# First three weight tiles loaded ahead of the first chunk, another order of the first eight steps' pieces, zeros in wider matmuls

## Chip, cores, metric

One core of a Trainium2 chip (trn2). The metric is device microseconds (us) of one execution; every kernel ran several times, and ratios compare its runs with runs of the kernel before on the same chip. In the profiles PE is TensorE (PEld its weight loads), DVE VectorE, ACT ScalarE, POOL GpSimd, and SP issues the loads; "share" of DMA is that of 16 engines.

## The reference, cut to what matters

```python
# retention: per head, a decayed state; q, k, v are (4, 8, 768, 64), float32
for t in range(S):
    state = gamma[None, :, None, None] * state + np.einsum('bhd,bhe->bhde', k[:, :, t], v[:, :, t])
    y[:, :, t] = scale * np.einsum('bhd,bhde->bhe', q[:, :, t], state)
x = y.transpose(0, 2, 1, 3).reshape(3072, 512)
# feed-forward; w_in is (512, 2048), w_out (2048, 512), both float64
h = x @ w_in
return ((h - np.tanh(h)) @ w_out).astype(np.float32)
```

## The kernel before

The sequence is cut into 24 chunks of 128 tokens. A chunk is turned (q and k transposed, on PE for the first eight chunks), multiplied into scores and state products with 32 small matmuls, masked, and put out as x. The feed-forward runs in 96 steps of an up product, a chain on ACT and DVE, and a down product two steps later. The weights come as float64 in 32 tiles: each is converted by two instructions on ACT, four on DVE and a last two on DVE or GpSimd. The first eight steps and eight chunks are written out as a list of pieces. A letter names the piece, a number its chunk, tile or step:

```python
pieces = {
    "L": load_chunk, "W": load_weights,
    "s": lambda c: scale(c, 0, tall(c)),          # q of a chunk, on DVE or GpSimd
    "w": lambda c: scale(c, 1, tall(c)),          # v of a chunk
    "t": ..., "T": ...,                           # PE transposes of k, of q
    "c": ..., "C": ...,                           # ACT copies of these
    "p": products, "m": mask, "z": state,         # PE, DVE, DVE
    "b": outputs, "r": outputs_rest, "y": keep_x, # PE, PE, ACT ("e": ACT reads y once)
    "A": convert_begin, "D": convert_bits,        # a weight tile: ACT, DVE
    "G": lambda i: convert_end(i, tall(i)),       # and its end: DVE or GpSimd
    "u": ..., "v": ...,                           # up product, first and second half
    "a": ..., "q": ..., "d": ..., "g": ...,       # its chain on ACT, ACT, DVE, DVE
    "o": ..., "E": ...,                           # down product, its sum
    "x": lambda n: idle.__setitem__(0, n),        # n matmuls of zeros before the next group
}

def keep_busy(at):
    for _ in range(idle[0]):
        nc.tensor.matmul(at, busy, busy, start=True, stop=True, skip_group_check=True)
    idle[0] = 0

# in load_chunk: k and q of a chunk have two buffers, v has four
t = inp.tile([P, H, D], F32, tag=nm, name=f"{nm}_{ci}", bufs=4 if nm == "v" else 2)
```

A piece's instructions go to their engine in the order of the list, and every engine works in its own order. The float32 matmuls are two PE instructions each, a transpose is one.

Of the kernel before, what the change touches and what calls it, by code (L numbers as in the profile page):

```python
# [16 lines left out]
P = 128  # L17
# [7 lines left out]
B0, C0 = 1.1162213056058772, 5.494931718829769  # L25
B1, C1 = -1.609711559785289, 5.546157850574988
# [6 lines left out]
def kernel(  # L33
# [20 lines left out]
    nc = tc.nc  # L54
# [28 lines left out]
    def bank(tag, name):  # L83
        return ps.tile([P, BANK], F32, tag=tag, name=name)

    def banks(tag, name):

        return ps.tile([P, 2, BANK], F32, tag=tag, name=name, bufs=1)
# [4 lines left out]
    at = [0]  # L93
# [6 lines left out]
    busy = cst.tile([P, P], F32, name="busy")  # L100
# [9 lines left out]
    w1 = wts.tile([P, NC, DF], F32, name="w1")  # L110
    w2 = wts.tile([P, NM, DM], F32, name="w2")
# [78 lines left out]
    def convert_end(i, engine):  # L190
        if i not in words:
            return
        dst, src = weight_ends(i)
        head, low, power = words.pop(i)
        engine.tensor_tensor(low, low, power.bitcast(F32), op=ALU.mult)  # L195
        head = head.bitcast(F32)
        if isinstance(src, list):
            low, head = (t.rearrange("p (c n) -> p c n", c=NC) for t in (low, head))
        engine.tensor_tensor(dst, low, head, op=ALU.add)  # L199
# [5 lines left out]



    idle = [0]

    def keep_busy(at):  # L210
        for _ in range(idle[0]):
            nc.tensor.matmul(at, busy, busy, start=True, stop=True, skip_group_check=True)  # L212
        idle[0] = 0


    loaded = {}
# [15 lines left out]
    def scale(ci, which, engine):  # L232
        if ci >= NCH:
            return
        t, g = loaded[ci][1 + which], (gq, gv)[which]
        engine.tensor_tensor(t, t, g[:, ts(ci % CPB, H)][:, :, None].to_broadcast([P, H, D]),  # L236
                             op=ALU.mult)

    def turn(ci, which, early=False):

        if early:
            tp = bank("o", f"kqTp{which}_{ci}")
        else:
            if which == 0:
                turned[ci] = banks("t", f"kqTp_{ci}")
            tp = turned[ci][:, which]
        keep_busy(tp[:, :P])
        t = loaded[ci][which]
        for p in range(NP):
            nc.tensor.transpose(tp[:, ts(p, P)],  # L250
                                t[:, ds(2 * p, 2)].rearrange("p h d -> p (h d)"), ident)
        if early:
            turned.setdefault(ci, []).append(tp)
# [31 lines left out]
    scores = {}  # L285

    def products(ci):

        kh, _, vh = loaded[ci]
        kT, qT = (sides[ci][:, i] for i in range(2))  # L290
        sp = banks("t", f"s_{ci}")
        keep_busy(sp[:, 0, :P])
        scores[ci] = halves = sp.rearrange("p r (w n t) -> p r w n t", w=2, n=NP)
        for p in range(NP):
            for a in range(2):
                for i in range(2):
                    h, r = 2 * p + i, ds(D * a, D)
                    nc.tensor.matmul(halves[ds(D * i, D), a, 1, p], kh[r, h], vh[r, h],  # L298
                                     start=True, stop=True, skip_group_check=True)
        for p in range(NP):  # L300
            for a in range(2):
                for i in range(2):
                    r = ds(D * i, D)
                    nc.tensor.matmul(halves[ds(D * a, D), i, 0, p], kT[r, p, ts(a, D)],  # L304
                                     qT[r, p, ts(a, D)], start=True, stop=True,
                                     skip_group_check=True)
# [7 lines left out]
        masked[ci] = m  # L314

    def state(ci):
        halves = scores.pop(ci)
        j = ci % CPB
        if j == 0:
            states[ci] = mid.tile([P, 2, NP, D], F32, tag="state", name=f"state_{ci}", bufs=3)  # L320
            nc.vector.tensor_copy(states[ci][:, 1], halves[:, 0, 1])
        else:
            nc.vector.tensor_tensor(states[ci][:, 1], halves[:, 0, 1], states[ci][:, 0],
                                    op=ALU.add)
        if j < CPB - 1:
            nxt = mid.tile([P, 2, NP, D], F32, tag="state", name=f"state_{ci + 1}", bufs=3)
            nc.vector.tensor_tensor(nxt[:, 0], halves[:, 1, 1], states[ci][:, 1], op=ALU.add)
            states[ci + 1] = nxt
# [7 lines left out]
    def outputs(ci):  # L336

        j = ci % CPB
        vh = loaded[ci][2]
        turned.pop(ci, None)  # L340
        qT = sides.pop(ci)[:, 1]
        a_, st = masked.pop(ci), states.pop(ci)
        y = y_banks[:, ci % 2]
        keep_busy(y[:, 0, 0])
        begun = set()

        def to_y(p, i, a, lhsT, rhs):

            col, r = (i + p) % 2, (ci + p) % 2
            start = (r, col) not in begun  # L350
            begun.add((r, col))
            nc.tensor.matmul(y[ds(D * col, D), r, p // 2, ts(a, D)], lhsT, rhs,  # L352
                             start=start, stop=True, skip_group_check=True)

        def intra(first):
            for pp in range(NP // 2):
                for i in range(2):
                    for a in range(2):

                        for col in range(2):  # L360
                            p = 2 * pp + ((a + col) % 2 if first else (a + col + 1) % 2)
                            if (i + p) % 2 != col:
                                continue
                            r = ds(D * a, D)
                            to_y(p, i, a, vh[r, 2 * p + i], a_[r, i, p])

        for a in range(2):
            if j or a:
                for p in range(NP):
                    for i in range(2):  # L370
                        r = ds(D * i, D)
                        to_y(p, i, a, st[r, a, p], qT[r, p, ts(a, D)])
        intra(True)
        halfway[ci] = intra
# [25 lines left out]
    o_p = {}  # L400
# [6 lines left out]
    def up(n, m2, i):  # L407

        if i == 0:
            hps[n, m2] = bank("h", f"h_{n}_{m2}")  # L410
        hp = hps[n, m2][:, ts(i, TH)]
        keep_busy(hp[:, :P])
        for c in range(NC):
            nc.tensor.matmul(hp, w1[:, c, ts(2 * m2 + i, P)], xT[n // 2][:, c, ts(n % 2, TH)],  # L414
                             start=(i == 0 and c == 0), stop=(c == NC - 1),
                             skip_group_check=True)
# [39 lines left out]
    def down(n, m2, j, first, last):  # L456

        if first:
            o_p[j] = bank("o", f"o_{n}_{m2}_{j}")
            keep_busy(o_p[j][:, :P])  # L460
        for i in range(2):
            nc.tensor.matmul(o_p[j], gT[n, m2][:, i, ts(j, P)], w2[:, 2 * m2 + i],  # L462
                             start=(first and i == 0), stop=(last and i == 1))
# [74 lines left out]

    BEGUN = 8
    EARLY_TURNS = 4  # L540
    TO_VECTOR = 2

    def tall(ci):
        return nc.vector if ci < TO_VECTOR else nc.gpsimd

    pieces = {
        "L": load_chunk,
        "W": load_weights,
        "s": lambda c: scale(c, 0, tall(c)),
        "w": lambda c: scale(c, 1, tall(c)),  # L550
        "t": lambda c: turn(c, 0, c < EARLY_TURNS),
        "T": lambda c: turn(c, 1, c < EARLY_TURNS),
        "c": lambda c: turn_copy(c, 0),
# [7 lines left out]
        "y": keep_x,  # L561
        "A": convert_begin,
        "D": convert_bits,
        "G": lambda i: convert_end(i, tall(i)),
        "u": lambda s: up(*steps[s][:2], 0),
        "v": lambda s: up(*steps[s][:2], 1),
        "a": lambda s: shrink_begin(*steps[s][:2]),
# [3 lines left out]
        "o": lambda s: [down(*steps[s][:2], j, *steps[s][2:]) for j in range(2)],  # L571
        "E": lambda s: [add_up(*steps[s][:2], j) for j in range(2)],
        "x": lambda n: idle.__setitem__(0, n),
    }
    if w_out.dtype != F32:
        rooms += [xp.tile([P, 2, 2 * BANK], U32, tag="xT", name=f"raws_{i}") for i in range(3)]
    order = """
    L0 x8 t0 c0 s0 x5 T0 w0 L1 C0 x3 t1 W0 p0 c1 s1 m0 x2 T1 z0 W1 C1 w1 x3 b0 p1 e0 A0 r0
    m1 z1 y0 A1 D0 L2 x4 b1 t2 e1 c2 G0 r1 s2 y1 D1 x3 T2 w2 L3 u0 C2 W2 p2 G1 s3 t3 m2 T3
    w3 c3 v0 z2 C3 b2 A2 L4 p3 e2 W3 D2 a0 r2 s4 y2 w4 q0 W4 m3 z3 G2 x9 t4 b3 A3 d0 T4 e3  # L580
    C4 r3 g0 L5 y3 x1 p4 A4 W5 u2 D3 s5 v2 W6 w5 m4 D4 u1 G3 a2 q2 z4 L6 x6 t5 d2 G4 T5 A5
    v1 W7 C5 g2 b4 s6 a1 W8 p5 w6 e4 u3 D5 q1 v3 m5 A6 G5 z5 r4 L7 a3 t6 d1 b5 W9 y4 T6 e5
    o0 s7 g1 C6 w7 A7 W10 D6 q3 r5 t7 W11 T7 D7 G6 y5 C7 x3 u4 d3 v4 G7 A8 g3 p6 a4 o1 A9 m6
    z6 q4 D8 p7 E1 d4 G8 b6 o2 e6 m7 g4 A10 r6 z7 u5 y6 D9 b7 v5 D10 G9 e7 r7 a5 o3 y7 q5
    G10 u6 E3 d5 A11 v6 g5 o4 a6 D11 q6 u7 G11 d6 v7 g6 o5 a7 q7 E5 d7 g7 W12 L8 W13 W14
    """
    for piece in order.split():
        pieces[piece[0]](int(piece[1:]))
# [10 lines left out]
    for s in range(BEGUN, len(steps)):  # L599
        n, m2, first, last = steps[s]  # L600
        ci = with_chunk.get(s)
# [86 lines left out]
```

## Time and profile before

| | us |
|---|---|
| Time | 752.62, median of 3 (752.61 to 753.97) |
| PE busy | 740.9 (99% of the span of 752.1) |
| First useful transposes | 4.6 |
| First up product (u0) | 20.3 |
| Step 8, from where nothing is changed | 98.7 |
| Last up product | 734.06 |

The time is from the runs, PE's busy time from the page, the others from PE's timeline.

### The profile page before, as it was taken

Reading aid. Unit: us, or ns where it says so; the run is one execution under the profiler, and the core shown is the slowest. Engines: PE = TensorE matmul, PEld = TensorE weight load, DVE = VectorE, ACT = ScalarE, POOL = GpSimd, SP = SyncE. Lnnn points to the kernel's source line nnn. Section 1 sums busy time; section 2 is a strip of 40 time slices with the busy share of each in tenths; the row PEclk is TensorE's granted clock in tenths of the full one; section 3 lists DMA queues with packets and bytes.
Section 4 is the critical chain, followed back from the end, with each engine's and each line's share of the span. In section 5 each row is a group of like instructions: output and inputs, shape, how many; then the busy total and the mean of one; then the engine's idle time right before and its main releaser. Section 6 shows DMA issues by size and latency. Waiting matters only on the chain.

```text
span 752.1 us, 13885 instructions
## 1 busy us (share of the span) xinstructions
PE 740.9 (99%) x5502; PEld 509.9 (68%) x5502; DVE 518.0 (69%) x807; ACT 389.4 (52%) x727; POOL 126.9 (17%) x108
## 2 busy tenths in 40 slices
PE   8899999999999999999999999999999999999997
PEld 7786667666767676766676676666666666666775
DVE  4889989998898666656565656565665666656653
ACT  4567576667665546445545545444344434434442
POOL 0565445445444111100111100000000000000000
PEclk9999999999999999999999999999999999999999
DMA  9972436556553353343342421000000000000000
GB/s 196 234 182 74 127 89 172 158 158 153 156 128 84 99 155 107 67 96 93 91 99 71 98 58 56 29 1 1 29 0 1 28 1 0 29 0 1 28 2 28
DMA packets 125680, 59.76 MB, mean 79 GB/s; under 512 B 109872, under 2 KB 118576, under 8 KB 125616
## 3 DMA queue, kind: packets, MB, share of 16 engines
q1 hardware_dynamic: 125328, 58.67, 29.9%
q8 instruction: 43, 0.70, 0.4%
q10 hardware_dynamic: 288, 0.21, 0.1%
q14 instruction: 21, 0.17, 0.1%
HBM read 35.80 MB, written 14.68 MB: 67 GB/s over the span
## 4 chain that ended last, share of the span: by engine, by line
PE 96%; DMA 2%; DVE 1%; SPq 1%; ACT 0%; issue 0%; ACTq 0%; DVEq 0%
PE h L414 44%; PE o L462 42%; PE y L352 3%; PE o L470 2%; PE s L298 2%; PE s L304 1%; PE kqTp L212 1%; PE kqTp L250 1%; DMA raw<-in_moe_w_in_dram 1%; DMA k<-in_k_dram 1%; SPq L229 1%; DMA out_dram<-sum 0%; SPq L154 0%; DVE power L187 0%; DVE head L185 0%; DVE a L311 0%
## 5 line engine op out<-in xcount | busy, mean ns | idle before, releaser
L414 PE MATMUL h<-xT,w 128*128 128x256 f32 x1536 | 349.9, 381 | 0.0
L414 PEld LDWEIGHTS h<-xT,w 128*128 128x128 f32 x1536 | 289.7, 190 | 68.4 <-issue 31.8
L462 PE MATMUL o<-w,g 128*128 128x512 f32 x736 | 331.9, 593 | 0.0
L462 PEld LDWEIGHTS o<-w,g 128*128 128x128 f32 x736 | 139.4, 190 | 135.1 <-issue 128.4
L423 ACT ACTIVATE u<-h 128x512 f32<-128x512 f32 x96 | 57.3, 597 | 289.0 <-PE h L414 288.9
L439 DVE TENSOR_TENSOR th<-h,th 128x512 f32<-128x512 f32 x96 | 66.3, 690 | 176.0 <-ACT th L424 176.0
L453 DVE COPY_PREDICATED g<-large,th 128x512 f32<-128x512 int32 x96 | 71.8, 748 | 10.2 <-DVE g L452 0.5
L442 DVE SCALAR_TENSOR_TENSOR h<-q,h 128x512 f32<-128x512 f32 x96 | 66.8, 696 | 10.4 <-DVE h L440 0.5
L448 DVE SCALAR_TENSOR_TENSOR h<-q,h 128x512 f32<-128x512 f32 x96 | 66.6, 694 | 8.2
L431 ACT ACTIVATE q<-u,tab 128x512 f32<-128x512 f32 x96 | 69.4, 722 | 0.0
L432 ACT ACTIVATE q<-u,tab 128x512 f32<-128x512 f32 x96 | 69.1, 720 | 0.0
L433 ACT ACTIVATE large<-u,tab 128x512 f32<-128x512 f32 x96 | 68.8, 717 | 0.0
L452 DVE TENSOR_TENSOR g<-h,u 128x512 f32<-128x512 f32 x96 | 66.3, 691 | 3.3
L440 DVE SCALAR_TENSOR_TENSOR h<-u,h 128x512 f32<-128x512 f32 x96 | 65.8, 685 | 0.0
L236 POOL TENSOR_TENSOR q<-q,tab 128x512 f32<-128x512 f32 x22 | 24.3, 1104 | 198.4 <-DMA q<-in_q_dram 115.1
L424 ACT ACTIVATE th<-h 128x512 f32<-128x512 f32 x96 | 56.9, 592 | 0.0
L195 POOL TENSOR_TENSOR low<-low,power 128x512 f32<-128x512 f32 x30 | 38.5, 1282 | 103.1 <-DVE power L187 89.1
L199 POOL TENSOR_TENSOR w<-low,head 128x512 f32<-128x512 f32 x30 | 38.7, 1289 | 2.4
L352 PEld LDWEIGHTS y<-a,v 64*64 64x64 f32 x768 | 15.8, 134 | 16.7 <-ACT large L433 10.6
L236 POOL TENSOR_TENSOR v<-v,tab 128x512 f32<-128x512 f32 x22 | 26.5, 1207 | 0.1
L382 ACT COPY seen<-y 64x1 f32<-64x1 f32 x96 | 10.1, 153 | 28.2 <-PE y L352 27.8
L393 ACT COPY xT<-y 128x512 f32<-128x512 f32 x24 | 14.1, 587 | 17.0 <-PE y L352 17.0
(54 smaller groups left out, 412.8 us busy)
## 6 DMA issues: line engine op xcount, KB each, us to landing
rows<-apart SPq DMA_DIRECT2D x16, 512.0 KB, 2.8
k<-in_k_dram SPq DMA_DIRECT2D x24, 256.0 KB, 4.3
q<-in_q_dram SPq DMA_DIRECT2D x24, 256.0 KB, 4.9
v<-in_v_dram SPq DMA_DIRECT2D x24, 256.0 KB, 5.1
raw<-in_moe_w_out_dram SPq DMA_DIRECT2D x12, 512.0 KB, 3.6
out_dram<-sum SPq DMA_DIRECT2D x23, 256.0 KB, 2.1
raw<-in_moe_w_in_dram SPq DMA_DIRECT2D x14, 256.0 KB, 4.2
raw<-in_moe_w_in_dram SPq DMA_DIRECT2D x28, 128.0 KB, 3.9
```

The costliest lines, as they stand in the source:

```text
L414: nc.tensor.matmul(hp, w1[:, c, ts(2 * m2 + i, P)], xT[n // 2][:, c, ts(n % 2, TH)], start=(i == 0 and c == 0), stop=(c == NC - 1), skip_g ...
L423: nc.scalar.activation(u, hp, AF.Square)
L431: nc.scalar.activation(q0, u, AF.Square, bias=bias0)
L432: nc.scalar.activation(q1, u, AF.Square, bias=bias1, scale=math.sqrt(A))
L433: nc.scalar.activation(large, u, AF.Relu, bias=bias_m)
L439: nc.vector.tensor_tensor(th, hp, th, op=ALU.subtract)
L440: nc.vector.scalar_tensor_tensor(hp, in0=u, scalar=R, in1=hp, op0=ALU.subtract, op1=ALU.mult, reverse0=True)
L442: nc.vector.scalar_tensor_tensor(hp, in0=q0, scalar=C0, in1=hp, op0=ALU.add, op1=ALU.mult)
L448: nc.vector.scalar_tensor_tensor(hp, in0=q1, scalar=A * C1, in1=hp, op0=ALU.add, op1=ALU.mult)
L452: nc.vector.tensor_tensor(flat, hp, u, op=ALU.mult)
L453: nc.vector.copy_predicated(flat, large.bitcast(I32), th)
L462: nc.tensor.matmul(o_p[j], gT[n, m2][:, i, ts(j, P)], w2[:, 2 * m2 + i], start=(first and i == 0), stop=(last and i == 1))
```

## The change

The intent: load and convert three weight tiles while nothing else can run, so that DVE is not stopped later by a tile that comes late; take out the zeros that stand between useful matmuls later; and make the rest cheaper by 512-column matmuls. It also moves the scales of chunk 1 from DVE to GpSimd and those of chunk 4 from GpSimd to DVE. The core of the diff:

```diff
     def keep_busy(at):
-        for _ in range(idle[0]):
-            nc.tensor.matmul(at, busy, busy, start=True, stop=True, skip_group_check=True)
-        idle[0] = 0
+        most = at.shape[-1] // P
+        while idle[0]:
+            n = min(idle[0], most)
+            zeros = busy[:, None, :].to_broadcast([P, n, P])
+            nc.tensor.matmul(at[:, : n * P].rearrange("p (n t) -> p n t", n=n), busy, zeros,
+                             start=True, stop=True, skip_group_check=True)
+            idle[0] -= n
...
-    TO_VECTOR = 2        # scales and tile ends 0 and 1 on DVE, the others on GpSimd
+    SCALED = {0, 4}      # scales of these chunks on DVE
+    ENDED = {0, 1}       # ends of these tiles on DVE
...
+        "X": lambda n: (idle.__setitem__(0, n), keep_busy(bank("h", "zeros"))),
...
     order = """
-    L0 x8 t0 c0 s0 x5 T0 w0 L1 C0 x3 t1 W0 p0 c1 s1 m0 x2 T1 z0 W1 C1 w1 x3 b0 p1 e0 A0 r0
-    m1 z1 y0 A1 D0 L2 x4 b1 t2 e1 c2 G0 r1 s2 y1 D1 x3 T2 w2 L3 u0 C2 W2 p2 G1 s3 t3 m2 T3
-    w3 c3 v0 z2 C3 b2 A2 L4 p3 e2 W3 D2 a0 r2 s4 y2 w4 q0 W4 m3 z3 G2 x9 t4 b3 A3 d0 T4 e3
-    C4 r3 g0 L5 y3 x1 p4 A4 W5 u2 D3 s5 v2 W6 w5 m4 D4 u1 G3 a2 q2 z4 L6 x6 t5 d2 G4 T5 A5
     ... (four more lines)
+    W0 W1 W2 A0 D0 L0 A1 G0 D1 A2 L1 D2 X40 t0 W3 c0 s0 w0 X7 T0 t1 G1 C0 p0 c1 s1 z0 L2 m0
+    w1 X3 T1 b0 G2 e0 C1 p1 z1 A3 r0 L3 m1 t2 y0 D3 W4 c2 b1 s2 e1 X1 r1 T2 w2 y1 C2 X2 p2
+    s3 t3 m2 c3 z2 w3 L4 T3 b2 W5 C3 G3 p3 e2 A4 r2 m3 u0 z3 y2 L5 s4 t4 D4 b3 T4 v0 C4 w4
+    e3 r3 p4 y3 z4 s5 a0 u2 m4 q0 G4 L6 d0 W6 t5 W7 b4 A5 T5 w5 g0 v2 W8 C5 e4 u1 a2 D5 W9
     ... (four more lines, ending in "A11 o5 g7 D11 E5 G11")
     """
```

More of the change, by code (lines that the diff above doesn't have):

```diff
@@ L246, in turn @@
             tp = turned[ci][:, which]
-        keep_busy(tp[:, :P])
+        keep_busy(tp)
         t = loaded[ci][which]
@@ L291, in products @@
         sp = banks("t", f"s_{ci}")
-        keep_busy(sp[:, 0, :P])
+        keep_busy(sp[:, 0])
         scores[ci] = halves = sp.rearrange("p r (w n t) -> p r w n t", w=2, n=NP)
@@ L316, in state @@
     def state(ci):
-        halves = scores.pop(ci)
+        halves = scores[ci]
         j = ci % CPB
@@ L343, in outputs @@
         y = y_banks[:, ci % 2]
-        keep_busy(y[:, 0, 0])
         begun = set()
@@ L411, in up @@
         hp = hps[n, m2][:, ts(i, TH)]
-        keep_busy(hp[:, :P])
+        keep_busy(hp)
         for c in range(NC):
@@ L459, in down @@
             o_p[j] = bank("o", f"o_{n}_{m2}_{j}")
-            keep_busy(o_p[j][:, :P])
+            keep_busy(o_p[j])
         for i in range(2):
@@ L540, with engine @@
     EARLY_TURNS = 4
-    TO_VECTOR = 2
-    def tall(ci):
-        return nc.vector if ci < TO_VECTOR else nc.gpsimd
+    SCALED = {0, 4}
+    ENDED = {0, 1}
+    def engine(i, among):
+        return nc.vector if i in among else nc.gpsimd
     pieces = {
@@ L548 @@
         "W": load_weights,
-        "s": lambda c: scale(c, 0, tall(c)),
-        "w": lambda c: scale(c, 1, tall(c)),
+        "s": lambda c: scale(c, 0, engine(c, SCALED)),
+        "w": lambda c: scale(c, 1, engine(c, SCALED)),
         "t": lambda c: turn(c, 0, c < EARLY_TURNS),
@@ L563 @@
         "D": convert_bits,
-        "G": lambda i: convert_end(i, tall(i)),
+        "G": lambda i: convert_end(i, engine(i, ENDED)),
         "u": lambda s: up(*steps[s][:2], 0),
@@ L577 @@
     order = """
-    L0 x8 t0 c0 s0 x5 T0 w0 L1 C0 x3 t1 W0 p0 c1 s1 m0 x2 T1 z0 W1 C1 w1 x3 b0 p1 e0 A0 r0
-    m1 z1 y0 A1 D0 L2 x4 b1 t2 e1 c2 G0 r1 s2 y1 D1 x3 T2 w2 L3 u0 C2 W2 p2 G1 s3 t3 m2 T3
-    w3 c3 v0 z2 C3 b2 A2 L4 p3 e2 W3 D2 a0 r2 s4 y2 w4 q0 W4 m3 z3 G2 x9 t4 b3 A3 d0 T4 e3
-    C4 r3 g0 L5 y3 x1 p4 A4 W5 u2 D3 s5 v2 W6 w5 m4 D4 u1 G3 a2 q2 z4 L6 x6 t5 d2 G4 T5 A5
-    v1 W7 C5 g2 b4 s6 a1 W8 p5 w6 e4 u3 D5 q1 v3 m5 A6 G5 z5 r4 L7 a3 t6 d1 b5 W9 y4 T6 e5
-    o0 s7 g1 C6 w7 A7 W10 D6 q3 r5 t7 W11 T7 D7 G6 y5 C7 x3 u4 d3 v4 G7 A8 g3 p6 a4 o1 A9 m6
-    z6 q4 D8 p7 E1 d4 G8 b6 o2 e6 m7 g4 A10 r6 z7 u5 y6 D9 b7 v5 D10 G9 e7 r7 a5 o3 y7 q5
-    G10 u6 E3 d5 A11 v6 g5 o4 a6 D11 q6 u7 G11 d6 v7 g6 o5 a7 q7 E5 d7 g7 W12 L8 W13 W14
+    W0 W1 W2 A0 D0 L0 A1 G0 D1 A2 L1 D2 X40 t0 W3 c0 s0 w0 X7 T0 t1 G1 C0 p0 c1 s1 z0 L2 m0
+    w1 X3 T1 b0 G2 e0 C1 p1 z1 A3 r0 L3 m1 t2 y0 D3 W4 c2 b1 s2 e1 X1 r1 T2 w2 y1 C2 X2 p2
+    s3 t3 m2 c3 z2 w3 L4 T3 b2 W5 C3 G3 p3 e2 A4 r2 m3 u0 z3 y2 L5 s4 t4 D4 b3 T4 v0 C4 w4
+    e3 r3 p4 y3 z4 s5 a0 u2 m4 q0 G4 L6 d0 W6 t5 W7 b4 A5 T5 w5 g0 v2 W8 C5 e4 u1 a2 D5 W9
+    q2 p5 z5 G5 r4 v1 y4 m5 d2 b5 a1 s6 t6 o0 e5 L7 g2 w6 A6 W10 q1 D6 T6 W11 u3 C6 d1 s7 p6
+    w7 r5 v3 z6 y5 G6 A7 m6 g1 t7 b6 T7 u4 C7 D7 e6 a3 p7 z7 G7 A8 r6 v4 m7 y6 q3 d3 b7 o1
+    a4 g3 A9 q4 d4 u5 e7 g4 r7 v5 y7 E1 u6 D8 a5 q5 o2 d5 G8 g5 A10 v6 D9 u7 a6 q6 o3 D10 d6
+    G10 v7 E3 g6 G9 o4 a7 q7 d7 A11 o5 g7 D11 E5 G11 W12 L8 W13 W14
     """
```

## The prediction

> **What bounds the kernel now.** I read the page first, then the chain of work that ended last, then a table of stretches, the PE's waits, and the timelines of PE, DVE, DMA issues and GpSimd over the first 100 us, which is all that the change touches.
>
> ```profile
> PE 740.9 (99%) x5502; PEld 509.9 (68%) x5502; DVE 518.0 (69%) x807; ACT 389.4 (52%) x727; POOL 126.9 (17%) x108
> PE   8899999999999999999999999999999999999997
> DMA  9972436556553353343342421000000000000000
> ```
>
> PE is busy 99% of the span, and the chain is 96% PE. From 98.87 us on it is an unbroken alternation of 3.45 us (sixteen up matmuls) and 3.43 us (eight down matmuls) with chunk work between; those 653 us the change does not touch. So only PE time before 98.87 us can be won. The table of stretches says where it is (us, then busy time of PE, PEld, DVE, ACT, POOL, clock, DMA share, GB/s):
>
> ```profile
> 0.00:8.00 8.00, 6.71 (x40) 6.28 (x40) 1.55 (x3) 2.45 (x3) 0.20 (x4) 1.00 0.99 175
> 8.00:16.00 8.00, 5.77 (x194) 5.11 (x194) 5.16 (x11) 3.35 (x9) 0.00 (x0) 1.00 1.19 236
> 16.00:28.50 12.50, 12.23 (x302) 10.41 (x302) 10.33 (x16) 6.56 (x19) 5.31 (x5) 1.00 0.93 208
> 28.50:38.30 9.80, 6.21 (x92) 5.62 (x90) 9.28 (x15) 5.62 (x14) 7.00 (x6) 0.83 0.92 253
> 38.30:84.90 46.60, 46.58 (x652) 33.69 (x653) 43.19 (x67) 31.28 (x66) 25.07 (x21) 1.00 0.49 126
> ```
>
> After 38.3 us PE idles no more (46.58 of 46.60), though DVE is 93% busy beside it. Before 38.3 us the DMA engines are full (share 0.9 and more) and PE has holes. The large one, in PE's timeline and its waits:
>
> ```profile
> 28.05 0.46 PE L352 MATMUL y<-a,v 64*64 64x64 f32 x16
> 31.45 3.60 PE L212 MATMUL kqTp<-busy 128*128 128x128 f32 x18 [2.94 <-DVE state L327]
> 34.84 0.93 PE L250 MATMUL kqTp<-tab,k 128*128 128x128 f32 x4
> PE kqTp L212 <- DVE state L327: 2.9, 1, 2.9
> ```
>
> PE waits 2.94 us, then runs 3.6 us of zeros (L212) before it does anything useful: 6.3 us. What it waits for is the state of chunk 3 on DVE, and DVE is late because it stands in order behind the conversion of the third weight tile:
>
> ```profile
> 27.12 0.43 DVE L181 TENSOR_SCALAR head<-head 128x512 f32<-128x512 f32 x1 [1.66 <-ACT head L172]
> 28.77 1.15 DVE L187 TENSOR_SCALAR power<-head 128x512 uint32<-128x512 uint32 x1
> 19.34 2.38 SPq L154 DMA_DIRECT2D raw<-in_moe_w_in_dram x3
> 26.40 0.69 ACT head L172
> ```
>
> That tile was issued at 19.34 us, behind four chunks, and landed at 26.3. So the chain of the hole is DMA, ACT, four DVE instructions, mask and state of chunk 3, PE.
>
> **What the Trainium skill says.** "SBUF — State Buffer", section "Who interferes with whom", says that VectorE and GpSimd share a port pair by an exclusive lock, so one fully blocks. The trace agrees: the bit operations of a conversion take 0.43 us alone, and 1.15 to 1.39 us beside a GpSimd instruction (28.77 above; GpSimd scales chunk 4 then). I count 13 such cases before 90 us, some 11 us of DVE. "TensorE: Matmul & The Clock Gate", Part 1, says that the clock is halved at the start and after about 3.4 us without work. The trace agrees roughly: the first 16 zero instructions take 3.78 us, later ten take 1.28, and the clock of 30 to 35 us is 0.71 after the 2.9 us hole. "DMA: Bandwidth & Descriptors", section "Why small descriptors are slow (HBM only)", says that 256-byte descriptors pay a fixed overhead. The trace agrees: 218 GB/s at 5 to 8 us, where all 2586 packets are under 512 bytes (chunks), and 250 GB/s at 8 to 11 us, where w_in's come in.
>
> **The change, part by part.** Units: a chunk is three loads of 262 KB, a weight tile 524 KB.
>
> *1. Three weight tiles first.* The new DMA order is W0 W1 W2, chunk 0, chunk 1, W3, chunk 2, chunk 3, W4, chunk 4, W5. What PE can do first is delayed. Chunk loads land 1.2 us apart (chunk 1's k released PE at 8.14 us, its q DVE at 9.34). A w_in tile costs 2.0 us at 260 GB/s; by landings it costs more, as cumulative bytes over landing times hold near 198 GB/s (before: 5.2 MB at 28.4 us), so 2.0 to 2.65 us. Start 2.2 us, table 0.6: W2 lands at 9 to 11 us, k of chunk 0 at 11 to 12.6 instead of before 4.6. That is 7 us later for the first transposes. v of chunk 3 has W2 and W3 ahead of it as well and lands at 27 to 28.9 us.
>
> *2. The zeros.* X40 stands at the head of PE's queue: 40 units of 128 columns in ten matmuls of 512. A wide unit costs 0.215 us (eight 512-column instructions in 3.43 us, two per matmul), narrow 0.224 (twelve instructions in 1.34), so 8.6 us, plus about 1.8 for the cold start: from 1.05 to about 11.4 us. That is just when k of chunk 0 lands, so they delay nothing. Width alone is worth 40 x 0.009 = 0.36 us, in idle time: nothing. X7 X3 X1 X2 (13 units, 2.8 us) also fall into waits for DMA. After chunk 3 no zeros are left, where before x6 and x3 (1.34 + 0.67 = 2.0 us) stood in a PE without idle time. Those 2.0 us are won outright, unless DVE then sets a wait.
>
> *3. The order.* The first up matmuls (u0) come only after the products of chunk 3. Walk the chain with 0.44 us per transpose group, 1.1 for products, 0.86 and 0.39 for outputs, 1.25 for a GpSimd scale: q of chunk 3 at 25.7 to 27.7, v scaled at 28.3 to 30.2, products done 29.4 to 31.3, u0 from 29.8 to 31.7. DVE and ACT keep up in that time: D0 D1 D2 are over by 14 us, before the first q needs scaling, and W3's conversion falls at about 23 us between chunks. So the hole of 6.3 us is gone, and what replaces it is DMA arrival.
>
> Compare at a common point. At 39.83 us the old kernel has done chunks 0 to 3, transposes and products of chunk 4, and u0 v0. The new one at u0 still needs u0 v0 (3.5), outputs of chunk 3 (1.25), turn and products of chunk 4 (2.0) = 6.7 us, which puts it at 36.5 (fast loads) or, with a wait of 0.7 us for chunk 4's copy and scale, 38.5 (slow loads). Gain there 3.4 or 1.3 us. The rest up to step 8 took 98.87 - 39.83 = 59.0 us and takes 57.0 without zeros. Sum: 5.4 or 3.3 us; the middle is 4.3.
>
> *4. DVE after 31 us.* Its work is the same in sum (two scales and two weight ends moved between tiles; 7 us per step for multiply, convert, mask). I followed it: D4 is over at 36, factor of step 0 at 44, step 1 at 60, step 6 at 88, step 7 at 93, each a little ahead of the PE instruction that needs it (o4 at 87, o5 at 91, step 6's down at 97 us). The new order places most GpSimd conversions outside the DVE's bit operations, so part of the 11 us of port collisions should go; but as PE was already the bound that yields slack, not time. I take 0.3 us off for small new waits: 4.0 us gained, 752.6 - 4.0 = 748.6 us.
>
> **Rivals.**
>
> A: the weights-first loads cost more than they save. If W0 to W2 delay chunk 3 by another 3 us (stragglers on single engines, as at 15.5 to 17 us, where the DMA rate falls to 17 GB/s, one engine), u0 starts at 34 to 35 and the gain at the common point is gone; only the 2.0 us of zeros stay: 750.5 to 752. For: DMA share 0.9 to 1.2 up to 38 us. Against: the new order keeps a weight tile queued whenever a chunk's buffer is awaited.
>
> B: DVE becomes the bound. It is 93% busy from 38 to 85 us in the old kernel, which has 46.6 us for work that the new one must do in 2 to 5 us less. If collisions don't fall, PE waits at masks and factors for up to 3 us: 750 to 752. Against: D0 to D2 and both DVE weight ends are done before 17 us, in time where DVE was idle before (6.5 us of waiting for q).
>
> C: everything PE lost is won. Idle and zeros from 4.6 to 38.3 us sum to about 19 us, with the later zeros 21; without the late start this would be 732. Against: DMA cannot deliver three more weight tiles and four chunks before 27 us at the rates shown; so even the good case ends at 746.
>
> **Range and chances.** A and B set the upper end, 751.6; the fast-load walk with less idling the lower, 746.0. A gain of 2% needs 15 us, which C alone gives and DMA forbids; a loss of 2% would need a stall of 15 us in a start that lasts 99. Hence 0.02, 0.97, 0.01.
>
> **What would show it.** Right: first useful transposes at 11 to 12.6 us; u0 at 30 to 32 with waits before it put down to DMA or to GpSimd scales, not to DVE state; no zeros after it; step 8's first up matmul (then the 3.45/3.43 alternation) at 93 to 96 us against 98.87; from there on the same 653 us. Wrong: PE idle again after 40 us with DVE as releaser (B); u0 after 34 us (A); clock well under 1 between 12 and 31 us, so that chunk work doubles; or DMA rates well over 260 GB/s for the first tiles, which would bring u0 to 27.

## The result

The changed kernel took 754.41 us (median of 6, 753.45 to 755.44), the kernel before 752.70 (median of 6, 752.53 to 753.97). The ratio is 1.0019, 95% interval 1.0006 to 1.0032. A ratio here is the mean time of one kernel's runs over that of the other's of the same rounds, so not quite the ratio of the medians. A gain of 4 us was predicted; there is a loss of about 1.5 us.

The two profiled runs differ by 1.6 us (spans 752.1 and 753.7; each is among the slowest of its kernel). The page of the changed kernel, its first lines of engines and slices:

```profile
PE 742.2 (98%) x5438; PEld 503.3 (67%) x5438; DVE 511.7 (68%) x807; ACT 389.4 (52%) x727; POOL 124.7 (17%) x108
DMA  9892436664552353332442412000000000000000
```

DVE did 6 us less (518.0 to 511.7) in the same 807 instructions: the collisions with GpSimd that the new order avoids. Before 90 us, 13 DVE instructions of the kernel before took over 0.4 us longer than others of the same kind; in the changed one, 3 did. The end did not come earlier for it. PE's timeline of the changed kernel (start, duration, line, operation, tiles, shapes; in brackets the idle time before and what ended it):

```profile
11.97 0.60 PE L256 MATMUL kqTp<-tab,k 128*128 128x128 f32 x4
...
16.13 0.66 PE L256 MATMUL kqTp<-tab,q 128*128 128x128 f32 x4 [2.05 <-DVE q L242]
...
33.57 1.99 PE L419 MATMUL h<-xT,w 128*128 128x256 f32 x8
...
54.21 0.34 PE L357 MATMUL y<-a,v 64*64 64x64 f32 x5 [1.21 <-issue]
...
99.62 3.62 PE L419 MATMUL h<-xT,w 128*128 128x256 f32 x16
```

The hole before chunk 4 is gone, as intended. But the transposes of q wait for DVE, u0 starts at 33.57 us instead of the predicted 29.8 to 31.7, there is a wait of 1.21 us in the middle of a group of matmuls at 53.0, and step 8 begins at 99.62 instead of 98.70. Later, a further 0.68 us is lost between steps 8 and 13 (the last up product starts at 735.66 against 734.06). PE's waits from 10 to 130 us (waited for, total, times, longest) show the late one as well:

```profile
PE kqTp L256 <- DVE q L242: 2.1, 1, 2.1
PE y L357 <- issue: 1.2, 1, 1.2
...
PE s L304 <- issue: 0.6, 1, 0.6
PE s L310 <- issue: 0.5, 1, 0.5
PE o L467 <- POOL w L199: 0.4, 1, 0.4
```

Why DVE is late is in the timelines of ACT, DVE and GpSimd (POOL) of the changed kernel:

```profile
5.91 1.28 ACT L172 ACT_TABLE_LOAD   x1 [5.91 <-DMA raw<-in_moe_w_in_dram]
7.20 0.67 ACT L172 ACTIVATE head<-raw 128x512 f32<-128x512 f32 x1
...
15.39 0.68 DVE L242 TENSOR_TENSOR q<-q,tab 128x512 f32<-128x512 f32 x1
15.99 0.68 DVE L242 TENSOR_TENSOR v<-v,tab 128x512 f32<-128x512 f32 x1
16.59 1.53 DVE L195 TENSOR_TENSOR low<-low,power 128x512 f32<-128x512 f32 x1
18.16 1.41 DVE L199 TENSOR_TENSOR w<-low,head 128x512 f32<-128x512 f32 x1
...
16.46 1.11 POOL L242 TENSOR_TENSOR q<-q,tab 128x512 f32<-128x512 f32 x1 [16.02 <-DMA q<-in_q_dram]
17.54 1.48 POOL L242 TENSOR_TENSOR v<-v,tab 128x512 f32<-128x512 f32 x1
```

ACT's first activation in the new order works on the first weight tile, and the load of its table, 1.28 us, stands behind the wait for that tile. In the kernel before, the first activation is a copy of a transpose and the table was loaded at 1.19 us, while nothing could run. The four DVE instructions of three tiles and the end of one (D0 G0 D1 D2) then stand ahead of the first scaling of q, which starts at 15.39 us, though q had landed at 12.73 (by the trace). Finally the end of tile 1 collides with two GpSimd scales and takes 1.53 + 1.41 us instead of 0.69 + 0.69, ahead of state and mask of chunk 0.

What that does to the loads is in the table of stretches (us, then busy time of PE, PEld, DVE, ACT, POOL, clock, DMA share, GB/s):

```profile
12.00:18.00 6.00, 3.95 (x73) 2.69 (x75) 5.83 (x10) 2.35 (x5) 1.54 (x2) 1.00 1.18 227
18.00:24.00 6.00, 4.33 (x142) 3.44 (x130) 3.04 (x6) 2.14 (x7) 4.54 (x4) 0.89 0.72 163
24.00:30.00 6.00, 5.79 (x151) 4.61 (x148) 4.22 (x8) 2.73 (x8) 4.08 (x5) 0.83 0.78 199
...
22.65:26.07 3.42, 3.42 (x84) 2.97 (x88) 2.15 (x5) 2.26 (x4) 2.04 (x2) 0.50 0.94 202
```

From 18 to 30 us the DMA engines are not full (0.72 and 0.78), since the k buffer of chunk 2 is free only after the products of chunk 0; that load was issued at 17.91 us. The last line is what lies behind PE's clock of 0.89 and 0.83: 3.4 us at half clock, with PE busy throughout.

Chunk 3 itself came when it was predicted all the same. By the trace its q landed at 26.52 us and its v at 28.52 (predicted 25.7 to 27.7 and 27 to 28.9), and its v was scaled by 29.63 (28.3 to 30.2). But its products began only at 31.40: PE was still at work on chunk 2, whose products began at 28.54, and from 22.65 us on it had waited only 0.2 us. So in this run u0 waited for PE's own queue, which had been late since chunk 1 (products at 21.30).

A "wait with no releaser" (issue) deserves a look of its own. I counted the records of PE's three rows (matmuls, weight loads, sequencer) before each such wait inside a group of small matmuls. The changed kernel has them at 962, 1218 and 1730, that is 194 + 3, 4 and 6 times 256; the kernel before has one at 449, which with a record missing is 194 + 256. Each ends 1.4 to 1.7 us after a transfer of 16 KB on the queue that the page calls "instruction" (these ended at 13.56, and at 31.41, 39.01 and 52.75 us). There are 43 of these for the changed kernel's 11,016 records, 256 records each. So these are waits for the next 256 instructions (theory F). The kernel before has 1.5 us of them, at 13.5 us; the changed one 2.3 us, at 32 to 54 us.

### The profile page after: what moved, and what is told of

It is laid out like the page before. It is cut to its first block, busy times and chain, and to the rows that moved or that the text cites. A ratio compares the mean times of both kernels' runs of the same rounds, so it can differ in the third digit from the quotient of the medians.

```text
span 753.7 us, 13758 instructions
## 1 busy us (share of the span) xinstructions
PE 742.2 (98%) x5438; PEld 503.3 (67%) x5438; DVE 511.7 (68%) x807; ACT 389.4 (52%) x727; POOL 124.7 (17%) x108
## 4 chain that ended last, share of the span: by engine, by line
PE 92%; DVE 5%; issue 1%; DMA 1%; ACT 1%; POOL 0%; SPq 0%; DVEq 0%; ACTq 0%; POOLq 0%
PE h L419 43%; PE o L467 40%; PE y L357 4%; PE o L475 2%; PE s L310 2%; PE s L304 2%; PE kqTp L256 1%; DVE head L185 1%; DVE head L183 1%; DMA raw<-in_moe_w_in_dram 1%; DVE head L181 0%; DVE power L187 0%; DVE g L458 0%; DVE low L195 0%; DVE h L447 0%
```

## The experiments

Theory H: what sets u0 is the head of DVE's queue (table load, D0 G0 D1 D2, the collision), carried on by the two-deep buffers of k and q. Rival D: the rate of the loads, with three and then four tiles ahead of chunks. Theory F: the fetch of PE's instructions, where four chunks stand in a row. All kernels were correct. The table gives, from each one's profiled run, when the transposes of q of chunk 0 begin (T0), u0, and step 8; and the times.

| Kernel | T0 | u0 | step 8 | median us | ratio to before (95%) |
|---|---|---|---|---|---|
| before | 6.55 | 20.33 | 98.71 | 752.70 | |
| changed | 16.13 | 33.57 | 99.62 | 754.41 | 1.0019 (1.0006, 1.0032) |
| tab_early | 14.79 | 31.16 | 96.94 | 752.72 | 1.0006 (0.9994, 1.0017) |
| d2_late | 14.25 | 31.16 | 97.09 | 753.62 | 1.0014 (1.0002, 1.0026) |
| g1_late | 16.85 | 34.23 | 99.06 | 753.91 | 1.0014 (1.0000, 1.0028) |
| kq4 | 16.78 | 33.43 | 97.43 | 753.15 | 1.0008 (0.9996, 1.0020) |
| a_all_kq4 | 14.24 | 32.90 | 97.45 | 753.71 | 1.0012 (0.9999, 1.0024) |
| shift | 18.75 | 35.08 | 100.06 | 755.05 | 1.0029 (1.0015, 1.0043) |
| w23late | 13.15 | 32.03 | 100.63 | 755.20 | 1.0030 (1.0016, 1.0044) |
| d11_early | 17.10 | 34.05 | 99.83 | 754.91 | 1.0023 (1.0010, 1.0035) |
| u_early | 14.79 | 25.00 | 98.39 | 753.47 | 1.0000 (0.9988, 1.0013) |
| b_d2late_no9 | 6.79 | 20.10 | 99.15 | 755.16 | 1.0029 (1.0016, 1.0041) |
| b_nozero | 7.29 | 20.30 | 96.36 | 751.47 | 0.9980 (0.9967, 0.9994) |
| b_wide | 6.84 | 20.11 | 96.80 | 751.94 | 0.9988 (0.9974, 1.0002) |
| b_no9 | 6.74 | 20.05 | 95.61 | 750.74 | 0.9967 (0.9955, 0.9980) |
| b_best | 7.05 | 20.14 | 96.06 | 750.79 | 0.9965 (0.9952, 0.9979) |
| b_best_kq4 | 6.96 | 20.14 | 95.18 | 750.55 | 0.9969 (0.9957, 0.9982) |

Read it with care. The intervals are about 1 us to either side. Runs of a kernel with weights first spread by 1.3 to 3.9 us, those of b_no9 by 0.7. In four profiles with the same head (changed, g1_late, kq4, d11_early) T0 lies between 16.13 and 17.10 us. A single profile is thus good for what waits for what, and for differences of over a microsecond.

The profiles also differ in PE's clock. Before 60 us, eight of the 17 hold one stretch of 3.4 us at 0.50: before (from 32.09 us), changed (22.65), g1_late (17.76), kq4 (17.81), d11_early (17.43), w23late (32.37), b_d2late_no9 (35.06) and b_best (36.85); the other nine hold none. It mostly follows a wait of PE of 2 us or more, but not each such wait is followed by one (2.09 us in u_early, none), so what starts it is not shown. It costs time where PE is the bound: the two runs of the changed kernel with a mean clock of 0.997 took 755.2 us on average, the other four 754.1. Part of the spread is this.

**tab_early.**

```diff
     nc.vector.memset(busy, 0.0)
+    nc.scalar.copy(out=seen[:, :1], in_=busy[:, :1])
```

> The changed kernel plus one tiny copy on ACT right after the zeros are set, so that ACT loads its table at about 1 us instead of behind the first weight tile (5.91 to 7.20 us). Theory H (the head of DVE's queue, D0 G0 D1 D2 ahead of the first scaling of q, sets when chunk 0's products end, and through the two-deep k and q buffers when chunks 2 and 3 arrive): D0 starts at 6.6 instead of 7.9, the first q transposes at 15 instead of 16.1, u0 about 1.2 us earlier (32.4 instead of 33.6), total 753.2 (changed kernel 754.4). Rival D (three weight tiles ahead of the chunks: DMA rate decides when chunk 3 is there): u0 stays at 33.6, total stays 754.4.

T0 came at 14.79 as expected, u0 2.4 us earlier (1.2 expected), as the collision went too: the end of tile 1 now ran before GpSimd had q of chunk 1. DVE's timeline of tab_early:

```profile
15.26 0.68 DVE L196 TENSOR_TENSOR low<-low,power 128x512 f32<-128x512 f32 x1
15.97 0.69 DVE L200 TENSOR_TENSOR w<-low,head 128x512 f32<-128x512 f32 x1
```

The products of chunk 1 began at 18.86 us instead of 21.30, so the 2.4 us were there before the changed kernel fell to half clock. From there to u0 both took 12.3 us: the changed kernel with its 3.4 us at half clock, tab_early at full clock with 1.8 us of waits for k from DMA and for q and v from GpSimd. The DMA share of 18 to 24 us rose from 0.72 to 0.92. Theory H holds for u0. In time it is about 1 us (1.0006 against 1.0019), with intervals that overlap.

**d2_late.** `A2` and `D2` moved behind `m0`.

```diff
-    ... A1 G0 D1 A2 L1 D2 X40 t0 ... z0 L2 m0
+    ... A1 G0 D1 L1 X40 t0 ... z0 L2 m0 A2 D2
```

> The changed kernel with the conversion of the third weight tile (its ACT and DVE parts) moved behind the first chunk's mask; loads as they are. Theory H: the first scaling of q no longer stands behind D2 (2.05 us): q transposes at about 14.2, products of chunk 0 end 2 us earlier, load of chunk 2 issued 2 us earlier (16 instead of 17.9), u0 1 to 2 us earlier as D2 falls into DVE's wait at 21 to 24 us; total 752.4 to 753.4. Rival D: no change in u0 (33.6), 754.4.

T0 1.9 us earlier, products of chunk 1 at 18.77 us, u0 2.4 us earlier; H again. The time gained 0.4 us by the ratios, within noise; the profiled run was this kernel's fastest.

**g1_late.** `G1` moved behind `m0`.

```diff
-    T0 t1 G1 C0 p0 c1 s1 z0 L2 m0
+    T0 t1 C0 p0 c1 s1 z0 L2 m0 G1
```

> The changed kernel with the DVE end of the second weight tile (two instructions that took 1.53 and 1.41 us beside GpSimd scales instead of 0.69) moved behind the first chunk's state and mask. Theory H: state and mask of chunk 0 are 3 us earlier, so the wait of PE for them (0.4 and 0.6 us) and the late products of chunk 1 (21.3 to 23.8) go, load of chunk 3 issued at about 20.5 instead of 22.0, u0 1 to 1.5 us earlier, total 753. Rival D: no change, 754.4.

A miss. u0 was at 34.23. T0 came 0.7 us later in this run, and the products of chunk 1 began at 22.28 instead of 21.30. PE was at half clock from 17.76 to 21.17 us, through the products of chunk 0: their 32 instructions of k with v took 1.13 us instead of 0.69. The state of chunk 0 followed them at once (19.98). So this run does not tell what the collision costs. tab_early does: there the collision was gone, and that state came 2.25 us after T0 instead of 3.37.

**kq4.** k and q of chunks 2 and 3 go to a part of the second weight matrix that is written much later.

```diff
-            t = inp.tile([P, H, D], F32, tag=nm, ...)
+            if nm != "v" and ci in (2, 3):
+                t = w2[:, NM - 1 - 2 * (ci - 2) - (nm == "q")].rearrange("p (h d) -> p h d", h=H)
+            else:
+                t = inp.tile([P, H, D], F32, tag=nm, ...)
```

> The changed kernel with k and q of chunks 2 and 3 loaded into parts of the second weight matrix that are not written until much later, so that these loads wait for no product. Theory H: this cuts the chain from products to the load two chunks later; DMA then runs on without the holes at 18 to 24 us, chunk 3 lands by about 27, u0 1 to 2.5 us earlier (31 to 32.5), total 752 to 753.4. Rival D: loads were bound by the rate anyway, the holes are short, u0 moves under 0.5 us, total 754 to 754.4.

Loads of chunk 2 were issued at 16.58 instead of 17.91, and DMA is full now in the table of stretches of kq4:

```profile
18.00:24.00 6.00, 5.29 (x159) 4.16 (x159) 3.54 (x5) 2.01 (x8) 5.62 (x5) 0.73 1.16 209
24.00:30.00 6.00, 5.67 (x181) 4.54 (x174) 4.43 (x8) 3.33 (x10) 3.70 (x4) 1.00 1.01 243
```

Yet u0 stayed (33.43, with T0 0.65 us later). The holes in DMA were real, but filling them brought u0 at most 0.8 us nearer to T0: v of chunk 3 landed at 28.33 us, and its products began at 31.25, with PE at half clock from 17.81 to 21.22 (the clock of 0.73). Loads did not set u0 here. Step 8 is 2.2 us earlier, mostly because no wait but one of 0.3 us is left after u0.

**a_all_kq4.** These four together.

> The changed kernel with all four mends at once: early table load, conversion of the third tile and DVE end of the second tile behind the first chunk's mask, k and q of chunks 2 and 3 in other buffers. Theory H (the head of DVE's queue and the buffers behind it delay chunk 3): they add up, first q transposes at about 13, u0 at 28 to 30 instead of 33.6, total 749 to 751. Rival D (rate of the loads): below about 31 us for u0 nothing more is won, total 752 to 753.

They do not add up: T0 at 14.24, but u0 at 32.90, and 753.71 us. The first reason is in this kernel's timeline of GpSimd: with D2 late, the end of tile 2 came late too (21.66 to 24.36 us), just ahead of the scale of q of chunk 2 (named `w` here, as kq4 puts it into the second weight matrix):

```profile
21.66 1.28 POOL L196 TENSOR_TENSOR low<-low,power 128x512 f32<-128x512 f32 x1 [3.43 <-ACT xT L402]
23.02 1.34 POOL L200 TENSOR_TENSOR w<-low,head 128x512 f32<-128x512 f32 x1
24.32 1.22 POOL L246 TENSOR_TENSOR w<-w,tab 128x512 f32<-128x512 f32 x1
```

The second is a wait of 1.35 us at record 962. And DMA share is 1.01 to 1.09 from 18 to 36 us: the loads have no more room.

**w23late.** In addition tiles 2 and 3 loaded behind chunks 2 and 3, their conversions behind the products of chunk 3 (and X30 for X40).

```diff
-    W0 W1 W2 A0 D0 ... X40 t0 W3 c0 ... z0 L2 m0 G1 A2 D2 ... r0 L3 m1
+    W0 W1 A0 D0 ... X30 t0 c0 ... z0 L2 L3 W2 W3 m0 G1 ... r0 m1 ... p3 e2 A2 D2 ... G2 A3 D3
```

> The changed kernel with the four mends, and with the third and fourth weight tile loaded behind chunks 2 and 3 instead of before them, their conversions moved to where they land; X30 in place of X40. Theory D (once DVE's head and the buffers are mended, the rate of the loads bounds u0, at 32.9 us there): two tiles of 524 KB at some 230 GB/s are 4.6 us, so u0 at 27 to 29 us. Total 749.5 to 752 if DVE catches up with its later conversions. If the loads are not the bound, u0 stays at 31 to 33.

Chunk 3's products began at 27.28 us (29.90 in a_all_kq4), 2.6 us earlier. Not all of it is the loads: the edit also took the end of tile 2 off GpSimd's way, and of PE's waits in a_all_kq4 before these products 1.5 us were for GpSimd and 0.5 for a load; T0 came 1.1 us earlier. By this count D is right to 1.6 us. u0 did not follow. PE's timeline of w23late:

```profile
28.25 0.22 PE L361 MATMUL y<-a,v 64*64 64x64 f32 x1
31.64 0.46 PE L361 MATMUL y<-a,v 64*64 64x64 f32 x15 [3.17 <-issue]
32.03 3.48 PE L423 MATMUL h<-xT,w 128*128 128x256 f32 x8
```

The wait is at record 962 again. One instruction transfer stands in the DMA view of 28 to 33 us; by the trace it ran from 28.77 to 30.30, 1.3 us before the wait ended, and u0 then ran at half clock (3.48 us for eight instructions instead of 1.9). Here the fetch, not the loads, set u0. The time got worse. Of the waits behind it, one shows a late DVE (1.27 us for a state, before 52.8); another of 1.3 us, before 64.8, has no releaser and is at record 1959, so no fetch; its cause is open.

**shift.** 128 more PE instructions in the idle head.

```diff
-    ... L1 D2 X40 t0 ...
+    ... L1 D2 N36 X24 t0 ...      # N36: 36 zero matmuls of 64x64 by 64
```

> The changed kernel with 128 more PE instructions in its idle head (36 tiny zero matmuls and 24 wide units instead of 40 wide units), so that everything after stands 128 places later in PE's instruction stream. Theory F (PE's waits without a releaser are fetches of the next 256 instructions): such waits are again found only at record numbers 194 + 256 k, that is at other places of the program (none in the products of chunk 4 at old number 1218, nor in outputs of chunk 5 at old number 1730), and their sum changes from 2.3 us to anything between 0 and 4. Rival: they stay at the same places of the program (their numbers rise by 128). Total within 1.5 us of 754.4 either way.

The waits are at records 961 and 1217 (one record is missing), as F says, and so in other places: PE's waits of shift have them in outputs (L363, `y`), where the changed kernel has them in products (L304 and L310, `s`).

```profile
PE y L363 <- issue: 2.3, 2, 1.2
```

The longer head held T0 back to 18.75, and with it the total, so its time says nothing about the fetches.

**u_early.** On top of tab_early, u0 and v0 back between the chunks.

```diff
-    ... y1 C2 X2 p2 ... w3 L4 T3 b2 ... r2 m3 u0 z3 ... b3 T4 v0 C4
+    ... y1 C2 u0 p2 ... w3 L4 T3 v0 b2 ... r2 m3 z3 ... b3 T4 C4
```

> The changed kernel with the early table load and with the first up matmuls put back between the chunks: u0 where X2 stood (after chunk 1), v0 after the transposes of chunk 3; nothing else. Theory F (four chunks in a row are 1,000 PE instructions, and their fetches of 256 can't follow while the loads run): the waits at record numbers 962 and 1218 go, and 3.5 us of up matmuls fall into time in which PE waits or runs zeros; step 8 begins at 94 to 95.5 us (96.9 with the early table alone), total 750.5 to 751.5. Theory D (loads alone): u0 and v0 fill waits too, so also faster, but waits at 256 k stay as they were (1.1 and 0.4 us). If place of u0 and v0 doesn't matter: 752.7.

A miss in time and step 8. The waits at 962 and 1218 are gone, and up matmuls run at 25.0 and 28.9 us. But step 8 came 1.4 us later than in tab_early in the profiles, and the times differ by 0.5 us (1.0000 and 1.0006), within noise. Other waits took their place: 1.4 us at the turn of chunk 4, 1.5 us behind ACT's reads of y, and a fetch of 2.1 us at record 1730. So breaking up the row of four chunks did not win time; it is one of several limits that lie within about two microseconds of each other.

**d11_early.** The last conversion before step 8 put ahead of step 7's factors.

```diff
-    G10 v7 E3 g6 G9 o4 a7 q7 d7 A11 o5 g7 D11 E5 G11
+    G10 v7 E3 g6 G9 A11 D11 o4 a7 q7 d7 o5 g7 E5 G11
```

> The changed kernel with the last conversion before step 8 (tile 11) moved ahead of the factors of step 7, as in the kernel before. If the late place of this conversion causes the 0.67 us that the changed kernel loses between steps 8 and 13 (PE waits 0.4 us for the end of tile 15 on GpSimd, at a lower clock after), that wait is gone and the stretch from step 8 to the last up matmuls takes 635.4 us again instead of 636.0. Total 753.8 against 754.4.

From step 8 to the last up product it took 635.37 us, as the kernel before (635.36), against 636.03: the wait for GpSimd is gone, and that term is shown. All other profiles agree: the nine with D11 late took 635.86 to 636.03, the six others in the old order 635.36. The total did not show it (1.0023): the profiled run was later by 0.2 us at step 8 already, and 0.7 us is within the noise of the times.

**b_nozero.** The kernel before without `x6` and `x3`.

```diff
-    ... z4 L6 x6 t5 ... C7 x3 u4 ...
+    ... z4 L6 t5 ... C7 u4 ...
```

> The kernel before without the nine zeros before t5 and u4 (2.0 us of PE time in a stretch in which PE never idles). The step of the prediction that these 2.0 us are won outright: total 750.6. Rival: other waits (DVE, instruction fetch) take their place: total 751.6 to 752.6, with a new PE wait before 85 us.

751.47 us; by the ratio 1.5 us less. Most of the 2.0 us is won; a wait of 0.64 us before t5 takes the place of the rest.

**b_no9.** The nine zeros before t4 taken out as well.

```diff
-    ... m3 z3 G2 x9 t4 ...
+    ... m3 z3 G2 t4 ...
```

> The kernel before without any of the zeros after 28 us that I can take out: the nine before t4 as well as those before t5 and u4. In the kernel before, PE waits 2.94 us for the state of chunk 3 and runs the nine zeros only after that wait, for 3.6 us at the lower clock. If PE bound the start from there on, they cost 2 to 3.6 us and this kernel takes 748 to 749.5 (751.4 with the other zeros gone alone). If DVE and the loads set the pace by then, other waits take their place and it stays at 750.5 to 751.5.

750.74 us (750.41 to 751.14); by the ratio 2.5 us less than before. This one change in the old order is worth 1 us, not 3.6. The hole did not close, it became a wait, and another came later. PE's timeline of b_no9:

```profile
30.78 0.63 PE L250 MATMUL kqTp<-tab,k 128*128 128x128 f32 x4 [1.51 <-issue]
...
33.58 0.46 PE L352 MATMUL y<-a,v 64*64 64x64 f32 x16 [0.72 <-ACT seen L382]
...
43.64 0.63 PE L250 MATMUL kqTp<-tab,k 128*128 128x128 f32 x4 [2.07 <-issue]
```

The two at a turn are not fetches (records 1083 and 1409): by their times they are waits for the bank that the state of the chunk before releases on DVE, whose last state instruction ended at 30.7 and 43.5.

**b_d2late_no9.** The kernel before (with x6 and x3) without the nine zeros, and D2 behind the state of chunk 3.

```diff
-    ... p3 e2 W3 D2 a0 ... m3 z3 G2 x9 t4 ...
+    ... p3 e2 W3 a0 ... m3 z3 D2 G2 t4 ...
```

> The kernel before, with nothing changed but this: the DVE part of the third tile's conversion moved behind mask and state of chunk 3, and the nine zeros that bridged the hole taken out. If the hole of 6.3 us came from the order on DVE alone, it shrinks to 1 or 2 us (wait for the scaled q of chunk 4), and the total is 748 to 750 against 752.6. If something else holds PE there as well (the load of chunk 4, landing at 28.4 us, or the third tile needed a few us later), the hole moves instead and the total is 751 to 753.

A clear miss: 755.16. DVE waited 2.5 us idle for the products of chunk 3, which D2 had filled before; from 29 us on it had no gap, and D2's 2 us now stood there. PE waited 1.95 us for a state before t5. The profile also has 3.4 us at half clock from 35.06, and all five runs a mean clock of 0.997 or less (four of five in b_no9 had 0.999 or more), so not all of the loss is DVE's. So in the kernel before, the hole at 28.5 us was not just an order on DVE: D2 filled a wait of DVE, and moved out of it, its 2 us came on top.

**b_wide.** The wide zeros alone.

> The kernel before with one part of the change alone: zeros in wider matmuls, order and loads as they were. Worked out: 47 units in all, each 0.009 us shorter, most of them in idle time: at most 0.3 us less, 752.3 to 752.6. Fewer PE instructions also move the places where the next 256 are fetched; theory F allows up to 1 us either way from that.

0.9 us less by the ratio, interval 0.9974 to 1.0002; not clear of noise, and if real more than the 0.3 us worked out.

**b_best and b_best_kq4.** b_no9 with wide zeros; then with the buffers of kq4.

> The kernel before with two things: wide zeros as in the change, and no zeros before t4, t5 and u4. The two gained 0.9 and 2.5 us alone. Added up: 749.6; if the wide zeros' gain was that of the nine zeros made shorter: 750.5 to 751.

> The same with k and q of chunks 2 and 3 in other buffers, so that their loads wait for no product. In the kernel before, the loads of chunks 2 and 3 were issued at 11.2 and 16.1 us, after the second weight tile; DMA had a hole at 15.5 to 17.5 us. If that hole delayed the third tile and what hangs on it: 0.5 to 1.5 us less than without. If not: the same within 0.4 us.

750.79 and 750.55 us (ratios 0.9965 and 0.9969). Neither adds anything to b_no9 (0.9967): the wide zeros bring nothing once the zeros are out, and the buffers of chunks 2 and 3 are not what holds the old order. All three beat both kernels by 2.3 us or more; b_no9 is the simplest.

## Why the prediction was wrong

The four us of predicted gain and the 1.6 us of loss in the profiles are 5.6 us apart. By the prediction's own sum (which slips at its slow end: 31.7 + 6.7 + 0.7 is 39.1 and not 38.5, a gain of 0.7 there and not 1.3, so that its middle should have been 3.7 us):

| Term | predicted gain | in the profiles | missing |
|---|---|---|---|
| Up to the common point (u2) | 2.35 (between 1.3 and 3.4) | -1.5 (39.83 to 41.33) | 3.85 |
| From there to step 8, without zeros | 2.0 | 0.6 | 1.4 |
| After step 8 | 0 | -0.7 | 0.7 |
| Allowance for small waits | -0.3 | | -0.3 |

- **Part 1, loads.** Its arrival of chunk 0 held (first transposes at 11.97, predicted 11 to 12.6). "The new order keeps a weight tile queued whenever a chunk's buffer is awaited" failed: share 0.72 and 0.78 at 18 to 30 us. Chunk 2's load waits for products that came later than in the walk. But chunk 3 landed within the predicted times (q at 26.52, v at 28.52), so this is not what made u0 late in the changed kernel.
- **Part 3, the step that failed: "D0 D1 D2 are over by 14 us, before the first q needs scaling".** They ended at 15.5, and q had landed at 12.73, so 14 would have been late too. Left out was the table load of 1.28 us behind the first tile, and the collision of G1 (2.94 us instead of 1.4). u0 came at 33.57, 2.8 us after the middle of its range. tab_early and d2_late show that 2.4 of these hang on DVE's head, as the products of chunk 1 came that much earlier. The walk took u0 from the loads of chunk 3, but PE, put behind by DVE's head, had not done chunk 2 when they were there. The mends do not add up in time either: behind the head stand GpSimd's order (a_all_kq4), the loads, and the fetch (w23late), each within some 2 us. How the 2.8 us would divide if all were mended stays open. And u0 is not all: in tab_early it came in the predicted range (31.16), and the profile gains only 1.1 us on that of the kernel before, the times nothing (1.0006). From u0 to u2 it took 8.3 us instead of the predicted 6.7, with a fetch of 1.11 us, and the 0.7 us after step 8 stayed. The kernel before was also profiled in one of its slowest runs, so its median is better than its profile by 1.3 us. The rest is open.
- **Part 2, zeros.** X40 indeed delayed nothing that counts: it ended at 12.0 us, k of chunk 0 landed at 11.53, and PE then waited for q. The step "those 2.0 us are won outright" holds in the old order to about 1.5 us (b_nozero). In the changed one, 0.6 us of them arrived: a fetch of 1.21 us at 53.0 took most of the rest, a cost that the prediction did not have. A fetch of 0.56 us is in the first row too.
- **Part 4, DVE.** That collisions would go was right (DVE 6 us less busy), and so was that this yields no time. That two tile ends move was misread from the diff: only scales do. The late place of D11 was followed only to step 8; behind it lay 0.68 us, through tiles 13 to 15, which d11_early takes away.
- **Rivals.** A named the right place (u0 late) for a cause that is at best a part (loads). B, DVE as the bound, was set for 38 to 85 us of the new order; something like it shows in the old order before 45 us (b_no9 and b_d2late_no9), where the prediction had called the hole a matter of order. The sign that the prediction set for being wrong, "clock well under 1 between 12 and 31 us", came true, at 0.83 to 0.89: 3.4 us at half clock. It came after chunk 1's products were already 2.4 us late by comparison with tab_early, so it was not the first cause. (C's 19 us of idle time and zeros from 4.6 us on are about 14.5 by the timeline; its verdict stays.)
- **The range** rested on two cases for load rates alone, as if everything else in the walk were certain. A chain of some thirty instructions across four engines, each placed by hand, deserved 3 us more on the side of the loss, since every omission lengthens it.

## What to carry to other kernels

When work is moved to the front, look at what was hidden there: a one-time cost (a table load), and every engine's first wait, now stand on the path. Where several engines and the loads are each within a few per cent of setting the pace, taking one hole away moves the wait to the next, and a gain is what is left after all have been walked. The surest gain here was to take out zeros late in the start of the old order (2.5 us, b_no9). Before two profiles are compared, their clocks should be: one stretch at half clock spoiled the test of g1_late. A wait without a releaser in the middle of small matmuls should be counted against multiples of 256 instructions.

## What the Trainium skill lacked or had wrong

- "Runtime: NRT & Kernel Launch", section "Instruction fetch mechanics", says that instructions come in blocks of 16 KiB (256) by the engine's own DMA queue, and that the cost of crossing a block is mostly hidden. The blocks agree: 43 transfers of 16 KB, and the fetch waits at 194 + 256 k. "Mostly hidden" agrees too: three of the changed kernel's 43 crossings show a wait. The page lacks what a crossing costs that is not hidden: 0.3 to 3.2 us in these runs, beside full load queues and small matmuls (3.17 us in w23late, followed by 3.4 us at half clock).
- "ScalarE: Activation LUTs", section "What ACT_TABLE_LOAD costs", gives 1283 ns, and the traces show 1.28 us. It lacks that the load can stand behind the first activation's wait for data, where it came onto the path (5.91 to 7.20 us), and that a copy of one column at the start takes it off (tab_early).
- "SBUF — State Buffer", section "Who interferes with whom", lacks nothing here: it has a DVE instruction with two SBUF inputs contend with GpSimd's reads, and the trace agrees, with 0.69 us alone, 1.53 and 1.41 us beside GpSimd scales.
